# A spectral filter and a gated FFN in one kernel: DRAM scratch rows in another order, forward slabs stored at once and put closer, block-product sums on VectorE

## The chip, the cores and the metric

The kernel runs on one core of one Trainium2 chip. The metric is device time in microseconds of one execution. The kernel before took 199.49 us as the median of three runs (199.12 to 199.73). The engines are named as in the profile: PE is TensorE (matmuls), PEld its weight loads, DVE is VectorE, ACT is ScalarE, POOL is GpSimd, and SP is SyncE, whose queue issues nearly all DMAs here.

## The reference: what is computed

```python
x  = A_x                                   # [1, 2048, 640] bf16
xn = layernorm(x)                          # over the last axis
X  = rfft2(xn) * (w_r + 1j * w_i)          # w_r, w_i: [2048, 321]
s  = irfft2(X)                             # [1, 2048, 640]
g  = silu((gelu(xn @ w_gate) * (xn @ w_up)) @ w_down)   # 640 -> 1536 -> 640
return x + s * g
```

## The kernel before, in words

The 2048 rows are 16 slabs (`NS`) of 128 rows: row = 16 * n2 + n1, with n1 the slab and n2 the partition. The spectral branch is a chain of matmuls with Fourier matrices.

- *Forward.* For each slab, `slab_S1` transforms along n2 (five matmuls into a PSUM tile `pz`, copied to SBUF by ScalarE), and `slab_D` transforms along the 640 columns (matmuls into `pd`, copied by ScalarE into one of six buffers of `RZ`). `slab_D` then stores the slab to the DRAM scratch `ZDR` (line 604).
- *Stage 2* needs the values of all 16 slabs for each frequency row, so `load_B2` reads `ZDR` back in another order, in ten loads (`B2`). `s2_in` transforms over the slabs (matmuls into `px`, line 647), ScalarE copies the result (`xs`, line 655), VectorE multiplies it by the two weights `W1` and `W2` into `RZ` (line 659). `s2_out` transforms back (matmuls into `pu`, line 674), ScalarE copies the result into `RX` in two parts (line 680), and after every second burst the rows are stored to the DRAM scratch `UDR` (line 683). There are eleven such bursts.
- *Inverse.* `load_V` reads `UDR` back as slabs (`VY` for the first four, `W2` for the rest, line 699). `gather` copies some columns (`vr`, line 710), `slab_S1i` transforms along n2 (`pv`, line 730), `group_Di` along the columns (`pd`, lines 575 and 579), VectorE forms the output rows, and `finish` multiplies by the gate, adds x and stores.

The FFN works on four groups of 512 rows. `ffn_half` is five matmuls of 512 columns with the gate weights (`psg`, then a gelu on ScalarE, line 811) or the up weights (`psu`, then a product on VectorE into `UT`, line 813). The down product of groups 1 and 2, and of half of group 3, is done with seven block products instead of eight per pair of row blocks (`product`, line 900): `u_sum` and `w_sum` form sums of blocks beforehand on VectorE, and behind each product the partial results are added (line 907). The other down products are plain (`down_third`, line 944). `gated` turns a down product into the gate, for groups 1 and 2 with a tanh on ScalarE and a multiply on VectorE, which is emitted one and two products later (`flush`).

`w_plus` and `w_minus` load the filter weights row by row into `W1` and `W2`.

The order of the work is written out by hand. The list `back` holds 144 steps of FFN work; `plan[s]` holds what is emitted right behind step s, by `put`. Steps 36 to 59 are the halves of FFN group 1 (even steps gate, odd steps up), 60 to 71 its block products (seven sixths of a product to a step), 72 to 95 and 96 to 107 the same of group 2, 108 to 131 the halves of group 3, 132 to 137 its block products, 138 to 143 the last plain ones. Every engine runs its own instructions in the order in which they are emitted, and the SP queue its DMAs. PSUM has two banks each for `psg` and `psu`, and two buffers of two banks shared by `pz`, `pd`, `px`, `pu` and `pv`.

Of the kernel before, what the change touches and what calls it, by code (L numbers as in the profile page):

```python
# [10 lines left out]
BF16 = mybir.dt.bfloat16  # L11
# [3 lines left out]
P = 128  # L15
# [17 lines left out]
def kernel(  # L33
# [27 lines left out]
    ZDR = dram.tile([2, 2, NS, 64, L], BF16)  # L61
    UDR = dram.tile([2, 2, NS, 64, L], BF16)
# [14 lines left out]
def build(nc, env):  # L77
# [32 lines left out]
    def w_plus(i, hh, lo):  # L110
        WT, sp = spw[i]
        p0 = hh * 64
        u0 = lo * 32 + hh * 16
        nc.sync.dma_start(out=WT[p0:p0 + 61:4, lo].rearrange("p h l -> p (h l)"),
                          in_=sp[:, u0:u0 + NS, :].rearrange("k h l -> k (h l)"))

    def w_minus(i, hh, lo):
        WT, sp = spw[i]
        p0 = hh * 64 + 1
        u0 = lo * 32 + hh * 16  # L120
        if u0 == 0:
            nc.sync.dma_start(out=WT[p0:p0 + 61:4, lo, 1:NS, :], in_=sp[:, 127:112:-1, :])
            nc.sync.dma_start(out=WT[p0:p0 + 61:4, lo, 0, :], in_=sp[:, 64, :])
        else:
            nc.sync.dma_start(out=WT[p0:p0 + 61:4, lo, :, :], in_=sp[:, 128 - u0:112 - u0:-1, :])
# [145 lines left out]
    def affine(name, src, a, b):  # L271
# [4 lines left out]
    kh_f, hi_f, s_f, h_f, pf, n1_f, z_f = bits(  # L276
        "pb", [(1, 31), (6, 1), (0, 31), (5, 1), (0, 127), (1, 15), (0, 1)])
# [14 lines left out]
    u64 = fma("u64", e64, 64.0, fma("u_f", z_f, 32.0, kh_f))  # L292
# [299 lines left out]
    def slab_D(n1):  # L592
# [10 lines left out]
        for a in range(2):  # L603
            nc.sync.dma_start(out=ZDR[a, :, n1].rearrange("c p l -> p c l"), in_=zd[a:P:2, :, 0:L])

# [9 lines left out]

    def load_B2():
        B2 = big.tile([P, NH, L], BF16, tag="sB", name="B2")
        zv = ZDR.rearrange("a c n (z k h) l -> (a c n z) k h l", z=2, k=2)
        B4 = B2.rearrange("p (k h) l -> p k h l", k=2)
        for h0, h1 in ((0, 3), (3, 6), (6, 9), (9, 12), (12, 16)):  # L620
            for hh in range(2):
                nc.sync.dma_start(out=B4[:, hh, h0:h1, :], in_=zv[:, hh, h0:h1, :])
# [3 lines left out]
        st_b["u"] = RX.rearrange("p b l -> p (b l)")[:, 0:2 * n_u].rearrange("p (s k x) -> p s k x", s=2, k=2)  # L626
# [11 lines left out]
    def s2_in(b):  # L638
# [3 lines left out]
        for lo in range(2):  # L642
            r = slice(64 * lo, 64 * lo + 64)
            for hh in range(2):
                for i, j, kind in s2_tiles(b, lo, hh):
                    ps = px[64 * hh:64 * hh + 64, lo, i * w:j * w].rearrange("p (h l) -> p h l", l=w)
                    nc.tensor.matmul(ps, lhsT=MG[r, kind, 0, :],  # L647
                                     rhs=B2[r, 16 * hh + h0 + i:16 * hh + h0 + j, l0:l0 + w], start=(i == 0),
# [13 lines left out]
    uv = UDR.rearrange("a c n (z k h) l -> (a c n z) k h l", z=2, k=2)  # L662

    def s2_out(b):
# [11 lines left out]
        us = st_b["u"][:, h0 // 3 % 2, :, 0:n * L].rearrange("p k (h l) -> p k h l", l=L)  # L676
# [4 lines left out]
        if l0 + w == L:  # L681
            for hh in range(2):
                nc.sync.dma_start(out=uv[:, hh, h0:h0 + n, :], in_=us[:, hh, :, :])
# [7 lines left out]
    def load_V():  # L691
# [4 lines left out]
        for V, n0, n1 in ((Va, 0, VA), (Vb, VA, NS)):  # L696
            for c in range(2):
                for a in range(2):
                    nc.sync.dma_start(out=V[a:P:2, :, c * L:c * L + L],
                                      in_=UDR[a, c, n0:n1].rearrange("n p l -> p n l"))  # L700
# [182 lines left out]
    TB = 3  # L883
# [7 lines left out]
    def product(g, a, i):  # L891
        if (a, i) == (0, 0):
# [4 lines left out]
                    (A(1, 0), TS[:, 2]), (S[:, 0], TS[:, 0]), (A(0, 1), B4[:, :, 1, 1, :]), (A(1, 1), TS[:, 3]))[i]  # L897
# [9 lines left out]
        add = lambda eng, out, in0, in1: eng.tensor_tensor(out=out, in0=in0, in1=in1, op=ALU.add)  # L907
# [3 lines left out]
        elif i == 1:  # L911
            c = temp()
            add(nc.vector, c, d["p1"], ps)
            gated(g, j, 0, c, True)
        elif i == 2:
            add(nc.vector, d["p1"], d["p1"], ps)
        elif i == 3:
            d["p7"], d["u3"] = temp(), temp()
            nc.scalar.copy(out=d["p7"], in_=ps)  # L919
            add(nc.gpsimd, d["u3"], d["p1"], d["p7"])  # L920
        elif i == 4:
            d["u4"] = temp()
            add(nc.vector, d["u4"], d["p1"], ps)
            add(nc.gpsimd, d["p7"], d["u4"], d["p7"])
        elif i == 5:
            add(nc.vector, d["p1"], d["u4"], ps)
# [133 lines left out]
    for i, at in enumerate((51, 52, 54, 56)):  # L1060
        put(at, w_sum, i)
    put(52, u_sum, nc.vector, 1, 0, 0, 3)
    put(57, u_sum, nc.vector, 1, 1, 0, 3)
    put(59, u_sum, nc.vector, 1, 0, 3, 6)
    for a, at in ((0, 86), (1, 92)):
        put(at, u_sum, nc.vector, 2, a, 0, 3)
    put(95, u_sum, nc.vector, 2, 0, 3, 6)
    put(122, u_sum, nc.vector, 3, 0, 0, 3)
    put(131, u_sum, nc.vector, 3, 0, 3, 6)
    F0 = 30  # L1070
# [21 lines left out]
    sb = z_end + 8  # L1092
# [5 lines left out]
    put(sb + 22, s2_out, len(BURSTS) - 1)  # L1098
    sb += 23
    put(sb, load_V)  # L1100
    vs0 = sb + 8
# [4 lines left out]
    for i, (n0, n) in enumerate(DG):  # L1106
# [3 lines left out]
        d = a + 6 if n == 3 else a + 3  # L1110
# [55 lines left out]
```

## Time and profile before

| | before |
|---|---|
| median of 3 runs | 199.49 us (199.12 to 199.73) |
| profiled execution | 198.94 us |
| its span, first to last instruction | 197.2 us |
| granted TensorE clock | 1.000 |
| busy VectorE / ScalarE / GpSimd | 158.4 / 127.6 / 48.9 us |
| moved by DMA | 32.44 MB |

In the lists of waits a row reads: engine and line that waited, what it waited for, then total us, how often, and the longest. In the timeline a row reads: start and length in us, engine, line, operation, output and inputs, and in brackets how long the engine had been idle in front of it and for what. Rows that begin with a stretch (82.00:95.00) give the length of the stretch and then the busy us of PE, PEld, DVE, ACT and POOL, the granted clock, the share of the DMA engines and GB/s. DMA rows end with KB of one and the median us from issue to landing.

### The profile page before, as it was taken

The page shows a single profiled execution, that of the slowest core. Times are in us where ns is not written, and L with a number is a line of the kernel's source. Part 1 is how long each engine was busy: PE and PEld are TensorE (multiplying, and loading weights), DVE is VectorE, ACT ScalarE, POOL GpSimd, SP SyncE. Part 2 cuts the span into 40 slices and gives each one's busy share as a digit, 9 for nine tenths or more (in the row PEclk, how much of TensorE's full clock was granted, in tenths as well). Part 3 has the DMA queues.
Part 4 walks back from the last instruction along what each step waited for, and adds up shares of the span by engine and source line. Part 5 has one row for each costly group of instructions (what it writes and reads, how often), then busy time and mean ns, then how long its engine had stood idle before and what let it go on. Part 6 is the DMA issues. An engine that isn't in the chain of part 4 may idle for free.

```text
span 197.2 us, 4191 instructions
## 1 busy us (share of the span) xinstructions
PE 188.7 (96%) x1496; PEld 116.4 (59%) x1511; DVE 158.4 (80%) x380; ACT 127.6 (65%) x229; POOL 48.9 (25%) x78
## 2 busy tenths in 40 slices
PE   7999999999999999999899999997999999999992
PEld 5798854777555555676433433454765555557672
DVE  7887888989899877697786658566779887978994
ACT  4668567866976666825598878622766738374761
POOL 4448588997210200032200000002120000000310
PEclk9999999999999999999999999999999999999999
DMA  6999999676596773329953222329910416040713
GB/s 162 301 331 362 367 320 188 139 207 208 134 179 126 218 243 104 99 72 317 243 132 103 76 100 100 116 69 257 325 41 28 138 41 195 33 136 15 220 44 94
DMA packets 39653, 32.44 MB, mean 165 GB/s; under 512 B 13264, under 2 KB 38608, under 8 KB 39376
## 3 DMA queue, kind: packets, MB, share of 16 engines
q1 hardware_dynamic: 37568, 29.87, 54.7%
q10 hardware_dynamic: 1968, 0.98, 1.8%
q0 software_dynamic: 96, 1.31, 1.7%
q8 instruction: 12, 0.20, 0.4%
q14 instruction: 9, 0.07, 0.1%
HBM read 19.03 MB, written 7.88 MB: 136 GB/s over the span
## 4 chain that ended last, share of the span: by engine, by line
PE 81%; DVE 8%; DMA 3%; issue 3%; ACT 2%; SPq 1%; DVEq 0%; ACTq 0%
PE psg L806 26%; PE psu L806 25%; PE psu L900 5%; PE psg L900 5%; PE psu L944 3%; PE psg L944 3%; PE pz L565 2%; PE pu L674 2%; PE pv L730 2%; PE pd L596 2%; PE pd L575 2%; DMA VY<-UDR 2%; PE px L647 2%; DMA X<-in_A_x_dram 2%; DVE X L788 1%
## 5 line engine op out<-in xcount | busy, mean ns | idle before, releaser
L806 PE MATMUL psg<-XG,Wg 128*128 128x512 bf16 (+2 forms) x282 | 60.1, 342 | 0.7 <-issue 0.3
L806 PE MATMUL psu<-XG,Wu 128*128 128x512 bf16 (+2 forms) x283 | 60.2, 342 | 0.4 <-issue 0.2
L813 DVE TENSOR_TENSOR UT<-psu,ge 128x512 bf16<-128x512 f32 (+2 forms) x58 | 34.4, 593 | 18.4 <-PE psu L806 16.1
L811 ACT ACTIVATE ge<-psg 128x512 bf16<-128x512 f32 (+2 forms) x58 | 30.3, 523 | 16.8 <-PE psg L806 16.1
L806 PEld LDWEIGHTS <-Wu 128*128 128x128 bf16 x290 | 27.0, 98 | 22.4
L806 PEld LDWEIGHTS <-Wg 128*128 128x128 bf16 x290 | 25.9, 98 | 21.3 <-issue 3.5
L659 DVE TENSOR_TENSOR RZ<-xs,W 128x972 bf16<-128x972 bf16 (+2 forms) x22 | 14.0, 678 | 5.5 <-ACT xs L655 4.7
L900 PEld LDWEIGHTS <-UT 128*128 128x128 bf16 x150 | 14.3, 98 | 5.6 <-issue 0.2
L944 PEld LDWEIGHTS <-UT 128*128 128x128 bf16 x156 | 14.4, 98 | 5.0
L601 ACT CAST RZ<-pd 128x660 bf16<-128x660 f32 x16 | 11.3, 707 | 9.1 <-PE pd L598 9.1
L190 DVE BATCH_NORM_STATS2 st<-X 128x6 f32<-128x320 bf16 x32 | 14.0, 476 | 0.4 <-DMA X<-in_A_x_dram 0.4
L732 ACT CAST W<-pv 128x640 bf16<-128x640 f32 x16 | 11.0, 688 | 5.0 <-PE pv L730 4.8
L755 ACT ACTIVATE W<-pd 128x960 bf16<-128x960 f32 (+2 forms) x14 | 10.0, 778 | 5.1 <-PE pd L579 5.1
L680 ACT CAST RX<-pu 128x486 bf16<-128x486 f32 (+4 forms) x22 | 12.2, 557 | 0.3
L655 ACT CAST xs<-px 128x972 bf16<-128x972 f32 (+2 forms) x11 | 10.3, 935 | 3.2 <-PE px L647 3.2
L944 PE MATMUL psg<-Wd,UT 128*128 128x320 bf16 (+1 forms) x84 | 11.8, 288 | 0.0
L567 ACT CAST GEN<-pz 128x640 bf16<-128x640 f32 x16 | 11.2, 698 | 0.0
L907 POOL TENSOR_TENSOR Tfwd<-Y,XG 128x320 f32<-128x320 f32 x1 | 0.9, 868 | 40.0 <-ACT XG L919 40.0
L844 ACT ACTIVATE th<-Tfwd 128x320 f32<-128x320 f32 x10 | 4.5, 469 | 9.5 <-DVE Tfwd L907 9.5
L907 POOL TENSOR_TENSOR Tfwd<-XG,Tfwd 128x320 f32<-128x320 f32 x1 | 0.9, 857 | 38.3 <-ACT Tfwd L919 38.3
L944 PE MATMUL psu<-Wd,UT 128*128 128x320 bf16 (+1 forms) x72 | 10.3, 290 | 0.0
L761 DVE TENSOR_TENSOR W<-W 128x960 bf16<-128x960 bf16 (+1 forms) x12 | 7.3, 632 | 1.8 <-ACT W L755 1.8
(215 smaller groups left out, 317.1 us busy)
## 6 DMA issues: line engine op xcount, KB each, us to landing
ZDR<-RZ SPq DMA_DIRECT2D x32, 80.2 KB, 2.8
UDR<-RX SPq DMA_DIRECT2D x10, 240.8 KB, 2.4
RX<-in_A_x_dram SPq DMA_DIRECT2D x14, 160.0 KB, 2.6
B<-ZDR SPq DMA_DIRECT2D x8, 240.8 KB, 4.3
W<-UDR SPq DMA_DIRECT2D x4, 481.5 KB, 7.1
X<-in_A_x_dram SPq DMA_DIRECT2D x3, 640.0 KB, 10.0
Wd<-in_B_w_down_dram SPq DMA_DIRECT2D x1, 1920.0 KB, 14.3
out_dram<-VY SPq DMA_DIRECT2D x12, 160.0 KB, 1.8
```

The source lines that it names most:

```text
L190: nc.vector.bn_stats(out=st_n[n1][:, k, :], in_=X[:, n1, 320 * k:320 * k + 320])
L567: nc.scalar.copy(out=Zt[n1], in_=pz)
L601: nc.scalar.copy(out=zd.rearrange("p c (q e) -> p c q e", e=10), in_=pd[:, :, 0:330].rearrange("p c (e q) -> p c q e", q=33))
L655: nc.scalar.copy(out=xs, in_=px[:, :, 0:n * w].rearrange("p k (h l) -> p k h l", l=w))
L659: nc.vector.tensor_tensor(out=pp[-1], in0=xs, in1=WT[:, :, h0:h0 + n, l0:l0 + w], op=ALU.mult)
L680: nc.scalar.copy(out=us[:, :, :, c0:c0 + (w + 1 - m) // 2], in_=pv[:, :, :, m:w:2])
L732: nc.scalar.copy(out=vs, in_=pv)
L806: nc.tensor.matmul(ps, lhsT=WT[:, c, t * P:(t + 1) * P], rhs=xnT[g][:, c, c0:c1_], start=(c == 0), stop=(c == 4))
L811: nc.scalar.activation(out=ges[t], in_=ps, func=ACT.Gelu_apprx_tanh)
L813: nc.vector.tensor_tensor(out=UT[:, t, c0:c1_], in0=ps, in1=ges[t], op=ALU.mult)
L900: nc.tensor.matmul(ps, lhsT=lhs[:, t, :], rhs=rhs[:, t, :], start=(t == 0), stop=(t == 5))
L944: nc.tensor.matmul(ph, lhsT=UT[:, t, j * P:(j + 1) * P], rhs=Wd[:, t, c0:c1_], start=(t == 0), stop=(t == NT - 1))
```

## The change

- The scratches `ZDR` and `UDR` lose the dimension that split odd and even rows. A scratch row index is now sign, half, row (`z a k`), so what stage 2 reads for one half lies together. A slab is stored by one transfer instead of two. `load_B2` and the `UDR` stores move 64 partitions with rows twice as long, instead of 128 partitions; `load_V` uses four transfers of 128 partitions instead of eight of 64.
- The constant `u64` and the weight loads follow the new order: `w_plus` now reads every second row, 16 pieces for a partition, where it read one long piece. `s2_in` reads every second row of `B2`. The two halves of the `RX` store buffer change places.
- The forward slabs (`FA`) stand closer behind step 43; the last `slab_D` and `load_B2` move from step 60 to 56. Stage 2 starts at step 67 instead of 68, `load_V` stays at 91, and the inverse starts at `vs0` = 98 instead of 99.
- In `product`, the fourth and fifth product change places. ScalarE's copy of one product and the two adds on GpSimd go; VectorE makes seven adds per pair instead of five.
- The sums in front of the products (`u_sum`) are made for five of six tiles at once before the last two halves, and for one tile behind them, instead of three and three.

```diff
-    ZDR = dram.tile([2, 2, NS, 64, L], BF16)
-    UDR = dram.tile([2, 2, NS, 64, L], BF16)
+    ZDR = dram.tile([2, NS, P, L], BF16)
+    UDR = dram.tile([2, NS, P, L], BF16)
...
-        u0 = lo * 32 + hh * 16
-        nc.sync.dma_start(out=WT[p0:p0 + 61:4, lo].rearrange("p h l -> p (h l)"),
-                          in_=sp[:, u0:u0 + NS, :].rearrange("k h l -> k (h l)"))
+        u0 = lo * 32 + hh
+        nc.sync.dma_start(out=WT[p0:p0 + 61:4, lo], in_=sp[:, u0:u0 + 31:2, :])
...
-    u64 = fma("u64", e64, 64.0, fma("u_f", z_f, 32.0, kh_f))
+    u64 = fma("u64", e64, 64.0, fma("u_f", h_f, 32.0, s_f))
...
-        for a in range(2):
-            nc.sync.dma_start(out=ZDR[a, :, n1].rearrange("c p l -> p c l"), in_=zd[a:P:2, :, 0:L])
+        nc.sync.dma_start(out=ZDR[:, n1].rearrange("c p l -> p c l"), in_=zd[:, :, 0:L])
...
+    def turned(t, lo, h0, h1):
+        return t[64 * lo:64 * lo + 64, 2 * h0:2 * h1, :].rearrange("p k l -> p (k l)")
+
+    def rows(t, lo, h0, h1):
+        v = t.rearrange("c n (z a k) l -> a (c n z) (k l)", a=2, z=2)
+        return v[lo, :, 2 * h0 * L:2 * h1 * L]
...
-            for hh in range(2):
-                nc.sync.dma_start(out=B4[:, hh, h0:h1, :], in_=zv[:, hh, h0:h1, :])
+            for lo in range(2):
+                nc.sync.dma_start(out=turned(B2, lo, h0, h1), in_=rows(ZDR, lo, h0, h1))
...
-                                     rhs=B2[r, 16 * hh + h0 + i:16 * hh + h0 + j, l0:l0 + w], start=(i == 0),
+                                     rhs=B2[r, 2 * (h0 + i) + hh:2 * (h0 + j) - 1 + hh:2, l0:l0 + w], start=(i == 0),
...
-        us = st_b["u"][:, h0 // 3 % 2, :, 0:n * L].rearrange("p k (h l) -> p k h l", l=L)
+        ut = st_b["u"][:, (h0 // 3 + 1) % 2, 0:2 * n, :]
+        us = ut.rearrange("p (h k) l -> p k h l", k=2)
...
-            for hh in range(2):
-                nc.sync.dma_start(out=uv[:, hh, h0:h0 + n, :], in_=us[:, hh, :, :])
+            for lo in range(2):
+                nc.sync.dma_start(out=rows(UDR, lo, h0, h0 + n), in_=turned(ut, lo, 0, n))
...
-                for a in range(2):
-                    nc.sync.dma_start(out=V[a:P:2, :, c * L:c * L + L],
-                                      in_=UDR[a, c, n0:n1].rearrange("n p l -> p n l"))
+                nc.sync.dma_start(out=V[:, :, c * L:c * L + L], in_=UDR[c, n0:n1].rearrange("n p l -> p n l"))
...
-    TB = 3
+    TB = 5
...
-                    (A(1, 0), TS[:, 2]), (S[:, 0], TS[:, 0]), (A(0, 1), B4[:, :, 1, 1, :]), (A(1, 1), TS[:, 3]))[i]
+                    (S[:, 0], TS[:, 0]), (A(1, 0), TS[:, 2]), (A(0, 1), B4[:, :, 1, 1, :]), (A(1, 1), TS[:, 3]))[i]
...
         elif i == 3:
-            d["p7"], d["u3"] = temp(), temp()
-            nc.scalar.copy(out=d["p7"], in_=ps)
-            add(nc.gpsimd, d["u3"], d["p1"], d["p7"])
+            d["u4"] = temp()
+            add(d["u4"], d["p1"], ps)
         elif i == 4:
-            d["u4"] = temp()
-            add(nc.vector, d["u4"], d["p1"], ps)
-            add(nc.gpsimd, d["p7"], d["u4"], d["p7"])
+            c, d["u3"] = temp(), temp()
+            add(c, d["u4"], ps)
+            gated(g, j + 1, 1, c, True)
+            add(d["u3"], d["p1"], ps)
...
         elif i == 6:
-            add(nc.vector, d["u3"], d["u3"], ps)
-            gated(g, j + 1, 1, d["p7"], True)
+            add(d["u3"], d["u3"], ps)
             gated(g, j + 1, 0, d["u3"], True)
...
-    for i, at in enumerate((51, 52, 54, 56)):
+    for i, at in enumerate((51, 52, 53, 54)):
         put(at, w_sum, i)
...
+    for g, at in ((1, 56), (2, 92), (3, 128)):
+        put(at, u_sum, nc.vector, g, 0, 0, TB)
+        if g in STR:
+            put(at + 1, u_sum, nc.vector, g, 1, 0, TB)
+        put(at + 3, u_sum, nc.vector, g, 0, TB, 6)
...
-    FA = (29, 31, 33, 35, 37, 39, 41, 43, 45, 47, 49, 51, 53, 55, 57, 58)
+    FA = (29, 31, 33, 35, 37, 39, 41, 43, 44, 46, 47, 49, 50, 51, 53, 54)
     for n1 in range(NS):
-        put(min(FA[n1] + 2, 45 + n1), slab_D, n1)
+        put(FA[n1] + 2, slab_D, n1)
         put(FA[n1], slab_S1, n1)
-    z_end = F0 + 30
+    z_end = FA[NS - 1] + 2
...
-    sb = z_end + 8
+    sb = 67
...
-    put(sb + 22, s2_out, len(BURSTS) - 1)
-    sb += 23
+    put(sb + 23, s2_out, len(BURSTS) - 1)
+    sb += 24
     put(sb, load_V)
-    vs0 = sb + 8
+    vs0 = sb + 7
...
-        d = a + 6 if n == 3 else a + 3
+        d = a + 6 if n == 3 else a + 4
```

More of the change, by code (lines that the diff above doesn't have):

```diff
@@ L119, in w_minus @@
         p0 = hh * 64 + 1
-        u0 = lo * 32 + hh * 16
+        u0 = lo * 32 + hh
         if u0 == 0:
-            nc.sync.dma_start(out=WT[p0:p0 + 61:4, lo, 1:NS, :], in_=sp[:, 127:112:-1, :])
+            nc.sync.dma_start(out=WT[p0:p0 + 61:4, lo, 1:NS, :], in_=sp[:, 126:97:-2, :])
             nc.sync.dma_start(out=WT[p0:p0 + 61:4, lo, 0, :], in_=sp[:, 64, :])
         else:
-            nc.sync.dma_start(out=WT[p0:p0 + 61:4, lo, :, :], in_=sp[:, 128 - u0:112 - u0:-1, :])
+            nc.sync.dma_start(out=WT[p0:p0 + 61:4, lo, :, :], in_=sp[:, 128 - u0:97 - u0:-2, :])
     def w_twin(i, pm):
@@ L274, in affine @@
         return t
-    kh_f, hi_f, s_f, h_f, pf, n1_f, z_f = bits(
-        "pb", [(1, 31), (6, 1), (0, 31), (5, 1), (0, 127), (1, 15), (0, 1)])
+    hi_f, s_f, h_f, pf, n1_f, z_f = bits("pb", [(6, 1), (0, 31), (5, 1), (0, 127), (1, 15), (0, 1)])
     cs_f = h_f
@@ L660, in s2_in @@
         st_b[b] = pp
-    uv = UDR.rearrange("a c n (z k h) l -> (a c n z) k h l", z=2, k=2)
     def s2_out(b):
@@ L906, in product @@
         j = 2 * a
-        add = lambda eng, out, in0, in1: eng.tensor_tensor(out=out, in0=in0, in1=in1, op=ALU.add)
+        add = lambda out, in0, in1: nc.vector.tensor_tensor(out=out, in0=in0, in1=in1, op=ALU.add)
         if i == 0:
```

19 lines of the change are left out of this document (4 added, 15 removed).

## The prediction

> **What bounds the kernel now.** I read the page first, then TensorE's waits, then the timeline around each wait.
>
> ```profile
> span 197.2 us, 4191 instructions
> ...
> PE 188.7 (96%) x1496; PEld 116.4 (59%) x1511; DVE 158.4 (80%) x380; ACT 127.6 (65%) x229; POOL 48.9 (25%) x78
> ```
> ```profile
> PE pv L730 <- DMA VY<-UDR: 1.3, 1, 1.3
> ...
> PE pu L674 <- ACT RX L680: 0.8, 2, 0.5
> ...
> PE pd L575 <- ACT W L732: 0.2, 1, 0.2
> ```
>
> TensorE is busy for 188.7 of 197.2 us. The change leaves its matmuls as they are, so a gain can only come out of TensorE's waits. Three of those lie near the change: 1.3 us for V (the slabs read back from UDR), 0.8 us where stage 2 opens, 0.2 us in the tail. A gain is at most 2.3 us, about 1.2%; a loss has no such bound.
>
> Two stretches of the timeline serve as rulers, one of stage 2 running and one where the inverse begins:
>
> ```profile
> 107.70 0.40 PE L647 MATMUL px<-B,MG 64*64 64x477 bf16 x4
> ...
> 108.15 0.96 ACT L655 CAST xs<-px 128x954 bf16<-128x954 f32 x1 [0.48 <-PE px L647]
> ...
> 109.14 1.23 DVE L659 TENSOR_TENSOR RZ<-xs,W 128x954 bf16<-128x954 bf16 x2 [0.57 <-ACT xs L655]
> ...
> 110.07 0.60 ACT L811 ACTIVATE ge<-psg 128x512 bf16<-128x512 f32 x1
> ...
> 110.71 0.40 PE L647 MATMUL px<-B,MG 64*64 64x486 bf16 x4
> ...
> 110.94 0.57 PE L674 MATMUL pu<-RZ,N 64*64 64x477 bf16 x8
> ```
>
> ```profile
> 133.71 0.98 PE L900 MATMUL psg<-X,XG 128*128 128x320 bf16 x6
> 134.53 0.22 PE L730 MATMUL pv<-Tinv,VY 128*128 128x128 bf16 x1
> 136.03 0.33 PE L730 MATMUL pv<-Tinv,VY 128*128 128x128 bf16 x3 [1.29 <-DMA VY<-UDR]
> ```
>
> A burst of stage 2 takes 3.01 us (107.70 to 110.71); px and pu fill 0.80 of it (110.71 to 111.51), so the two FFN halves between take 1.1 us each. A block product takes 0.82 us (133.71 to 134.53).
>
> **The change part by part.** The sums are made against the profiled execution, 198.94 us, which lies 0.55 us below the median of the runs shown (199.49). The difference is put on the median at the end.
>
> *Forward slabs closer, one store each.*
>
> ```profile
> 79.61 0.70 ACT L567 CAST GEN<-pz 128x640 bf16<-128x640 f32 x1
> ...
> 80.37 0.60 ACT L811 ACTIVATE ge<-psg 128x512 bf16<-128x512 f32 x1
> ```
> ```profile
> 82.65 0.41 PE L596 MATMUL pd<-FT,GEN 128*128 128x132 bf16 x4
> ...
> 83.17 0.71 ACT L601 CAST RZ<-pd 128x660 bf16<-128x660 f32 x1
> ```
> ```profile
> 72.91 12.41 SPq L604 DMA_DIRECT2D ZDR<-RZ  x16
> 87.38 4.79 SPq L622 DMA_DIRECT2D B<-ZDR  x10
> ```
> ```profile
> B<-ZDR SPq DMA_DIRECT2D x8, 240.8 KB, 4.3
> ```
> ```profile
> 90.38 0.79 PE L647 MATMUL px<-B,MG 64*64 64x162 bf16 x5
> ```
>
> The last slab's matmul (slab_D of 15) moves from step 60 to step 56. That is one product and three FFN halves earlier on TensorE, so about 4 us: it would run near 78.9 instead of 82.65. In the dense stretch ScalarE evicts two banks per slab (0.71 and 0.70) and a gelu every second step (0.60). From step 49 to 56 that is 11 evictions and 4 gelus, 10.2 us, beside about 12 us of TensorE; it fits, and the two PSUM buffers are each free before their next use. The tightest place is slab 12's first matmul group, which needs the last fold just as VectorE ends it: 0 to 0.2 us lost, I take 0.1.
>
> SyncE issues the old stores back to back, 16 in 12.41 us, so 0.6 to 0.8 us each and partly waiting. Sixteen fewer in all free about 10 us of that queue, which is off the path. The last store then leaves at about 80 and the first load of B2 at about 83 instead of 87.38. A landing of 4.3 gives 87.9 for the first pair. px of burst 0 moves one product earlier, to about 89.5, so the cover is 1.6 us: price nothing. If that cover goes, px waits, and everything behind it on TensorE.
>
> The weights' w_plus loads become 256 rows of 642 bytes in place of 16 long ones. They are read first in stage 2, tens of us later: nothing.
>
> *Stage 2 opens one step earlier, with all sums on VectorE.*
>
> ```profile
> 82.00:95.00 13.00, 13.00 (x110) 8.93 (x108) 11.19 (x24) 5.84 (x12) 3.10 (x4) 1.00 0.60 188
> ```
> ```profile
> 91.55 0.95 ACT L655 CAST xs<-px 128x972 bf16<-128x972 f32 x1
> ...
> 92.53 1.91 DVE L659 TENSOR_TENSOR RZ<-xs,W 128x972 bf16<-128x972 bf16 x2 [0.80 <-DMA B<-ZDR]
> ...
> 94.76 0.47 DVE L907 TENSOR_TENSOR FT<-Tfwd,psu 128x320 f32<-128x320 f32 x1
> ...
> 95.95 0.47 ACT L844 ACTIVATE th<-Tfwd 128x320 f32<-128x320 f32 x1 [3.13 <-DVE Tfwd L907]
> ...
> 96.33 0.94 ACT L655 CAST xs<-px 128x954 bf16<-128x954 f32 x1
> ...
> 97.16 1.17 ACT L680 CAST RX<-pu 128x486 bf16<-128x486 f32 x2
> ...
> 98.38 0.60 PE L674 MATMUL pu<-RZ,N 64*64 64x159 bf16 x10 [0.51 <-ACT RX L680]
> ```
>
> Before, ScalarE stood 3.13 us in front of a tanh whose sum VectorE had not made. xs of burst 1 (96.33) sat behind it, RX of burst 0 behind that, and pu at 98.38 waited for the buffer. Per pair of row blocks the change takes one 320-wide copy from ScalarE and two adds from GpSimd, and gives VectorE two adds more (seven for five). In the stretch 82 to 95 VectorE has 11.19 of 13 us, and gets 4 adds x 0.47 = 1.9 us. About 0.8 us of u_sum work moves ahead of it, since five sixths instead of one half is formed before the products. That makes 12.3 of 13: nearly full.
>
> I follow the new order: px of burst 0 ends near 90.3, xs (0.95) and the two multiplies (1.23, as in the bursts that run) end near 92.8; pu of burst 0 stands three products after px, near 93.1, and need not wait. xs of burst 1 has one tanh in front of it, whose sum is made by then, so the old wait goes. What is late next is burst 2. In front of its xs stand RX (to 95.5), three tanh (3 x 0.47) and a gelu (0.60), two of the tanh behind sums that VectorE makes after burst 1's multiplies. xs of burst 2 starts at 97.5 to 98.4, and its multiplies end at 99.7 to 100.6. Its pu is due near 99.6. The stall is 0.1 to 1.0 us against 0.8 before; I take 0.8, the end where sums do lag as they did, so no change. Bounds for the part: a gain of 0.8, or a loss of 1.9 if all the added VectorE time lands on the path.
>
> *Stage 2 running.*
>
> In the rows of the running bursts xs starts 0.45 after px; the multiplies end at 110.37, 0.57 before pu at 110.94. With the shift by one step, px stands behind a gate half instead of an up half. So ScalarE does the gelu (0.60) before xs, which starts about 0.65 after px, 0.2 later. The slack falls from 0.57 to about 0.37 and the period stays: price 0. Each 0.1 us beyond the slack would cost 0.1 in each of nine bursts.
>
> *V.*
>
> ```profile
> 126.51 1.47 SPq L683 DMA_DIRECT2D UDR<-RX  x1
> 130.57 2.62 SPq L699 DMA_DIRECT2D VY<-UDR  x4
> ```
> ```profile
> VY<-UDR SPq DMA_DIRECT2D x4, 160.5 KB, 3.1
> ```
>
> TensorE reaches the inverse at 134.53 and stands 1.29 us for the last of four loads, each about 0.65 us of issue (2.62 / 4). The change makes two of the four, so the last goes out about 1.3 us earlier; each carries twice the bytes, which gives part of it back (0.3 to 0.6). Burst 9's UDR store also leaves one step earlier and no longer runs into burst 10's, whose second issue took 1.47 us. That may bring the first load forward by up to 1 us. Against this the inverse starts one product earlier (134.53 - 133.71 = 0.82). V comes 0.7 to 2.0 earlier than it did, the need 0.82 earlier; but a wait of 1.29 that starts 0.82 earlier and ends 0.7 to 2.0 earlier still means TensorE goes on 0.7 to 1.29 earlier. I take 1.0. Bounds: 0 if loads land no sooner, 1.29.
>
> The copies of V into vr stand one product earlier in VectorE's queue and block it until V lands. TensorE has four banks to run ahead into, and only one product lies between: nothing.
>
> *Tail.*
>
> ```profile
> 179.35 0.36 DVE L881 TENSOR_TENSOR XG<-UT 128x384 bf16<-128x384 bf16 x1
> ...
> 180.28 0.49 DVE L788 TENSOR_TENSOR VY<-VY,XG 128x640 bf16<-128x640 bf16 x1
> ...
> 182.14 0.55 DVE L881 TENSOR_TENSOR UT<-UT,XG 128x768 bf16<-128x768 bf16 x1
> ...
> 185.69 0.87 POOL L907 TENSOR_TENSOR Tfwd<-Y,XG 128x320 f32<-128x320 f32 x1 [40.04 <-ACT XG L919]
> 185.87 1.21 DVE L770 TENSOR_TENSOR X<-W 128x960 bf16<-128x960 bf16 x1
> 186.21 0.46 PE L575 MATMUL pd<-FI,W 128*128 128x160 bf16 x4 [0.15 <-ACT W L732]
> ```
> ```profile
> 180.00:190.00 10.00, 9.85 (x95) 7.02 (x93) 9.76 (x22) 6.73 (x13) 2.03 (x2) 1.00 0.39 115
> ```
>
> VectorE has 9.76 of 10 us here, TensorE 9.85: both carry the tail. After the last gelu product the change adds two adds (0.95). It shortens three u_sum pieces: between 384 and 768 elements an operation grows by 0.19, so 128 elements cost about 0.23, three save 0.4. One slab's finish (two of 0.49) falls ahead of it, as the inverse is one step earlier. An add on GpSimd beside which an operation took 1.21 us is gone; how much of that it caused I leave out. The sum is about -0.4, so VectorE follows TensorE. The wait of 0.15 goes too, since ScalarE loses a copy in front of that eviction.
>
> **Sum:** forward +0.1, stage 2 0, V -1.0, tail -0.15: -1.05 us. On the profiled execution that is 197.9; on the median 199.49 - 1.05 = 198.4.
>
> **The rivals.**
>
> 1. *No measurable change.* The loads of V land no sooner, because they carry the same bytes and start behind the same last store. Then only 0.1 to 0.5 us is left: 199.0 to 199.8. For it: the four old loads were issued within 2.62 us and the last landed 3.1 after, so size may rule rather than count. Against it: two loads are issued in half the time.
>
> 2. *All three waits go.* -2.2 us, 197.3. For it: GpSimd's adds, ScalarE's copy and the tanh queue in front of xs are lighter. Against it: VectorE is full there.
>
> 3. *Slower, by transfers over half the partitions.* B2's loads now fill 64 partitions each, with rows twice as long. If their landing doubles (8.6 instead of 4.3), the first pair, issued at 83 to 83.6, lands at 92.2, px of burst 0 waits 2.7 us, and the UDR stores slow V too: about 201.5. It decides from a landing of 5.9 on. For it: the cover is only 1.6 us. Against it: the first pair has the queue to itself. [...]
>
> 4. *Slower, by VectorE where stage 2 opens.* If the sums lag more than about 1 us beyond my chain, xs and the multiplies of bursts 0 to 2 all come late and the 1.9 us land on the path: 199.49 - 1.05 + 1.9 = 200.3.
>
> **How the numbers follow.** The forecast's own case 0.38, with 197.9 to 198.9 (V's bounds); rival 1 0.20; rival 2 0.12; rival 3 0.12; rival 4 0.18. A change under 0.3%, 0.6 us, cannot be told from none here. Faster: 0.38 + 0.12 = 0.50. Same: 0.20. Slower: 0.30. The range must hold 8 in 10: from below rival 2's 197.3 to beyond rival 4's 200.3, leaving out most of rival 3: 197.1 to 200.8.
>
> **What would show it.** Right: TensorE's wait at pv under 0.5 us; a wait of about 0.8 us at pu of burst 2 and none at pu of burst 1; bursts still 3.01 us apart; px of burst 0 waiting for no DMA; no wait in the dense slabs. Wrong: a wait of px on B2 (rival 3); waits of more than 1.5 us around the first three bursts, or a period above 3.1 (rival 4); a wait at pv still above 1 us (rival 1).

## The result and the profile after

The changed kernel takes 196.54 us (median of four runs, 196.30 to 197.35) beside 199.31 us (199.00 to 199.73): a ratio of 0.9867, interval 0.9832 to 0.9902, 2.8 us faster. The forecast of 198.4 had the direction and less than half of the size; the time lies below the range. On three other chips the same kernel later gave 0.9946, 0.9897 and 0.9927. The mean of the four ratios is 0.991, about 1.8 us, so the first measurement was the most favourable one. The other three ratios, times 199.49, give 197.4 to 198.4, inside the forecast's range: that the time fell below the range is owed in part to the chip that was measured. A step of the prediction was wrong all the same (see below). Of the traced executions used later, one (no_layout) had a granted clock of 0.991 and took 200.47 us, 2.7 above that kernel's median; it is not read.

The profiled execution is the one of 197.35 us, the slowest of the four. The head of its page, and TensorE's waits in it (total us, times, longest):

```profile
span 195.6 us, 4175 instructions
...
PE 188.2 (96%) x1496; PEld 116.1 (59%) x1511; DVE 159.9 (82%) x391; ACT 126.6 (65%) x224; POOL 40.1 (20%) x68
```
```profile
PE pu L674 <- ACT RX L681: 0.4, 1, 0.4
PE pv L729 <- DMA VY<-UDR: 0.4, 1, 0.4
...
PE pz L563 <- DMA Tfwd<-Tinv: 0.3, 1, 0.3
```

The wait at pv fell from 1.3 to 0.4 us, that at pu from 0.8 to 0.4, and pd's is gone. A wait of 0.3 at pz, in the forward part, is new. GpSimd lost 8.8 us of work, VectorE took on 1.5.

The timeline where stage 2 opens (start, us, engine, line, operation; in brackets the idle time before it and what ended it):

```profile
89.84 0.41 PE L649 MATMUL px<-B,MG 64*64 64x162 bf16 x5
...
92.72 0.40 PE L649 MATMUL px<-B,MG 64*64 64x159 bf16 x5
...
93.18 0.96 ACT L657 CAST xs<-px 128x954 bf16<-128x954 f32 x1 [1.45 <-PE px L649]
...
94.70 1.23 DVE L661 TENSOR_TENSOR RZ<-xs,W 128x954 bf16<-128x954 bf16 x2
...
96.51 0.57 PE L674 MATMUL pu<-RZ,N 64*64 64x159 bf16 x10
...
98.91 1.16 ACT L681 CAST RX<-pu 128x480 bf16<-128x480 f32 x2
...
100.13 0.63 PE L674 MATMUL pu<-RZ,N 64*64 64x486 bf16 x8 [0.44 <-ACT RX L681]
```

Three things differ from before. px of burst 0 takes 0.41 us for its five matmuls, where it took 0.79. xs of burst 1 starts as px ends, with ScalarE idle in front of it, where it stood behind a tanh. pu of burst 1 (96.51) does not wait; the only wait left is at pu of burst 2.

The timeline at the start of the inverse, and in the tail:

```profile
128.60 1.11 SPq L699 DMA_DIRECT2D VY<-UDR  x2
...
132.97 0.22 PE L729 MATMUL pv<-Tinv,VY 128*128 128x128 bf16 x1
133.61 0.34 PE L729 MATMUL pv<-Tinv,VY 128*128 128x128 bf16 x3 [0.43 <-DMA VY<-UDR]
```
```profile
183.57 0.98 PE L899 MATMUL psg<-X,UT 128*128 128x320 bf16 x6
...
184.39 0.45 PE L573 MATMUL pd<-FI,W 128*128 128x160 bf16 x4
184.76 0.25 PE L577 MATMUL pd<-FI,W 32*128 32x160 bf16 x4
185.05 1.79 PE L942 MATMUL psg<-Wd,UT 128*128 128x320 bf16 x12
```

The two loads of V are issued 2 us earlier (128.60 for 130.57), the inverse starts 1.6 us earlier (132.97 for 134.53). pd follows its product after 0.82 us, where it was 1.14 before (186.21 - 185.07).

**One ledger for all traces.** The list of waits leaves out short losses. So I took, from each trace, the time between the starts of two successive matmuls, less the usual time for a matmul of that form, and summed it by stretch. "Early" is 6 to 42 us, "stage 2" 88 to 130 (some 2 us of it is a regular pause of about 0.2 in each burst), "pv" 130 to 138, "tail" from 176. In the traces that miss matmul records (the first of both kernels among them) a missing record looks like a loss of 0.2; only traces with all 1511 are in the table, but for the kernel before, whose values have the missing ones taken out (stage 2: the 3.17 of again3 plus 1.02, by which it falls behind that trace between the product at 87.84 and the FFN half at 126.14). The ledger leaves out the first 6 us and what follows the last matmul.

| kernel | ratio to before, same chip | early | stage 2 | pv | tail |
|---|---|---|---|---|---|
| before | 1 | 0.3 | 4.2 | 1.58 | 0.99 |
| layout alone | 0.9987 [0.9971, 1.0004] | 0.30 | 4.26 | 0.87 | 0.98 |
| sums alone | 0.9936 [0.9915, 0.9956] | 0.43 | 3.84 | 1.69 | 0.66 |
| places alone | 0.9959 [0.9940, 0.9979] | 0.43 | 3.47 | 1.22 | 0.66 |
| no_sums | 0.9917 [0.9890, 0.9943] | 0.33 | 3.48 | 0.32 | 0.66 |
| changed, again | 0.9946 [0.9928, 0.9965] | 0.69 | 3.17 | 0.91 | 0.75 |
| changed, again3 | 0.9927 [0.9898, 0.9956] | 0.32 | 3.17 | 0.45 | 0.75 |
| b2_late | 0.9903 [0.9879, 0.9928] | 0.61 | 3.17 | 0.00 | 0.75 |
| s2_late | 0.9958 [0.9937, 0.9978] | 0.57 | 3.77 | 0.43 | 1.45 |
| first_v | 0.9905 [0.9880, 0.9929] | 0.32 | 3.16 | 0.00 | 0.75 |
| before_no_v | 0.9947 [0.9926, 0.9968] | 0.62 | 4.46 | 0.00 | 0.98 |
| after_no_v | 0.9874 [0.9856, 0.9892] | 1.09 | 3.16 | 0.00 | 0.75 |

The stretches stage 2 and tail repeat to 0.01 us wherever the code there is the same and no transfer is waited for; early and pv do not, since they hang on transfers. From before to the changed kernel (again3) the gain is 1.0 in stage 2, 1.1 at pv and 0.24 in the tail. For the first pair of traces it is 1.0, 0.76 and 0.24, less 0.34 lost early, chiefly at pz; their spans differ by 1.6 us.

### The profile page after: what moved, and what is told of

Read it like the earlier page. It is cut to its first block, busy times and chain, and to the rows that moved or that the text cites. A ratio compares the mean times of both kernels' runs of the same rounds, so it can differ in the third digit from the quotient of the medians.

```text
span 195.6 us, 4175 instructions
## 1 busy us (share of the span) xinstructions
PE 188.2 (96%) x1496; PEld 116.1 (59%) x1511; DVE 159.9 (82%) x391; ACT 126.6 (65%) x224; POOL 40.1 (20%) x68
## 4 chain that ended last, share of the span: by engine, by line
PE 84%; DMA 7%; SPq 2%; DVE 2%; ACT 2%; issue 1%; DVEq 0%; ACTq 0%
PE psu L805 26%; PE psg L805 25%; PE psg L942 5%; PE psg L899 4%; PE psu L942 4%; PE psu L899 3%; DMA B<-ZDR 3%; PE psg L609 2%; PE pz L563 2%; DMA VY<-UDR 2%; PE pd L573 2%; PE pv L729 2%; SPq L624 2%; PE pd L594 2%; PE pu L674 2%
## 5 line engine op out<-in xcount | busy, mean ns | idle before, releaser
L805 PEld LDWEIGHTS <-Wu 128*128 128x128 bf16 x290 | 26.1, 98 | 22.5 <-issue 3.4
L805 PEld LDWEIGHTS <-Wg 128*128 128x128 bf16 x290 | 26.6, 98 | 20.1 <-issue 0.2
L661 DVE TENSOR_TENSOR RZ<-xs,W 128x972 bf16<-128x972 bf16 (+2 forms) x22 | 13.3, 648 | 9.8 <-ACT xs L657 9.5
L942 PEld LDWEIGHTS <-UT 128*128 128x128 bf16 x156 | 14.5, 98 | 5.1
L681 ACT CAST RX<-pu 128x486 bf16<-128x486 f32 (+4 forms) x22 | 12.3, 560 | 0.3
L942 PE MATMUL psg<-Wd,UT 128*128 128x320 bf16 (+1 forms) x84 | 11.8, 288 | 0.0
L942 PE MATMUL psu<-Wd,UT 128*128 128x320 bf16 (+1 forms) x72 | 10.3, 291 | 0.0
L207 POOL TENSOR_TENSOR rst<-ve,mhalf 128x1 f32<-128x1 f32 (+1 forms) x6 | 5.5, 913 | 11.5 <-DVE ve L205 11.5
L899 PE MATMUL psu<-Wd,UT 128*128 128x320 bf16 x48 | 7.8, 300 | 0.0
L594 PEld LDWEIGHTS <-GEN 128*128 128x128 bf16 x64 | 5.1, 98 | 3.3
## 6 DMA issues: line engine op xcount, KB each, us to landing
UDR<-RX SPq DMA_DIRECT2D x10, 240.8 KB, 3.1
B<-ZDR SPq DMA_DIRECT2D x8, 240.8 KB, 5.1
```

What stands on the lines that cost most here:

```text
L661: nc.vector.tensor_tensor(out=pp[-1], in0=xs, in1=WT[:, :, h0:h0 + n, l0:l0 + w], op=ALU.mult)
L681: nc.scalar.copy(out=us[:, :, :, c0:c0 + (w + 1 - m) // 2], in_=pv[:, :, :, m:w:2])
L805: nc.tensor.matmul(ps, lhsT=WT[:, c, t * P:(t + 1) * P], rhs=xnT[g][:, c, c0:c1_], start=(c == 0), stop=(c == 4))
L899: nc.tensor.matmul(ps, lhsT=lhs[:, t, :], rhs=rhs[:, t, :], start=(t == 0), stop=(t == 5))
L942: nc.tensor.matmul(ph, lhsT=UT[:, t, j * P:(j + 1) * P], rhs=Wd[:, t, c0:c1_], start=(t == 0), stop=(t == NT - 1))
```

## The experiments

The diff has three parts that can be taken alone: *layout* (the scratch's order, the one-transfer stores and loads), *sums* (the body of `product`, `TB`, the places of `w_sum` and `u_sum`) and *places* (`FA`, `z_end`, `sb`, `vs0`, `d`).

**Each part alone, beside the changed kernel.** Edits against the kernel before, cut to a line or two each:

```diff
 layout
-    ZDR = dram.tile([2, 2, NS, 64, L], BF16)
+    ZDR = dram.tile([2, NS, P, L], BF16)
...
 sums
-            add(nc.gpsimd, d["u3"], d["p1"], d["p7"])
+            add(d["u3"], d["p1"], ps)
...
 places
-    sb = z_end + 8
+    sb = 67
...
```

> The changed kernel once more, for its spread and a second trace. The runs seen so far are 197.35 (the profiled one), 196.30, 196.58 and 196.49. Theory: the profiled run was held up once, by the wait of 0.3 us of pz on the turned matrix (0.42 us against the kernel before) and by a longer wait at pv (0.4); a second trace then shows neither, a span of 194.5 to 195.0, and a time of 196.3 to 196.7. Rival: these waits are always there and only the other runs differ by chance; then the trace shows the two waits again and a span near 195.6.

> The kernel before with the DRAM layout alone: one store for a forward slab, loads of B2 and V in two transfers over 64 partitions; places and sums as before. Theory (the gain came from fewer transfers on SyncE's queue): the loads of B2 go out before 85 in place of 87.4, the hidden wait in px of burst 0 (0.79 us for 0.41) goes, 0.4 us; V's loads end sooner, 0.5 to 1.3 us; together 0.9 to 1.7 us faster, 197.6 to 198.4. Rival A (the same bytes land no sooner, the gain came from the places and sums): within 0.3 us of the kernel before. Rival B (half the partitions are slower): slower than the kernel before by more than 0.3 us.

> The kernel before with the sums alone: every add on VectorE, the new order of products, the new pieces of u_sum; layout and places as before. Theory: the tail's wait of 0.2 us at pd and VectorE's 0.4 us there give 0.25; where stage 2 opens the waits at pu fall from 0.8 to 0.4 or stay; together 0.2 to 0.7 us faster, 198.6 to 199.1. Rival (VectorE becomes the bound there): a wait of more than 1 us at pu, 199.6 or more.

> The kernel before with the places alone: the last forward slabs closer, B2's loads after the last of them, stage 2 and the inverse one step earlier; two stores for a slab and the old sums stay. Theory: the loads of B2 still stand behind 32 store issues, so they go out at 84 to 87 and px of burst 0, which now runs earlier, waits 0 to 1.5 us for them; the wait for V grows by the 0.8 us that the inverse is earlier, net nothing: 199.0 to 200.3. Rival (the places made the gain): 1 us or more faster, 198.3 or less.

Measured: again 197.58 us, layout 198.37, sums 197.08, places 197.85, beside 198.35 for the kernel before on that chip. The trace of again is as its rival said, with both waits and a span of 195.7, but its times (196.90 to 198.05) are 1 us above those of the first chip, which neither theory said. For the layout alone its rival A is right, in time: nothing measurable, though its trace shows 0.7 us less at pv. The sums gained 1.3 us by the medians, almost twice the most that their theory allowed; their traced execution, the slowest of nine, has a span only 0.9 us under that of the kernel before. The places did more than their theory, less than the rival. On this chip the sums alone (197.08) came out faster than the whole change (197.58), though the intervals of the two ratios overlap.

In the layout's trace (timeline), the last matmuls of px of burst 0 stand by themselves, because TensorE waited in front of them:

```profile
90.21 0.40 PE L649 MATMUL px<-B,MG 64*64 64x162 bf16 x3
90.99 0.40 PE L649 MATMUL px<-B,MG 64*64 64x486 bf16 x2 [0.38 <-DMA B<-ZDR]
```

This is the 0.79 us of the kernel before, seen apart: a wait for B2 of 0.4 us which a group of matmuls had covered up. With the places alone (timeline) it is gone, and pu of burst 1 no longer waits either; what is left is pu of burst 2:

```profile
89.59 0.40 PE L647 MATMUL px<-B,MG 64*64 64x162 bf16 x5
...
96.26 0.57 PE L674 MATMUL pu<-RZ,N 64*64 64x159 bf16 x10
...
100.19 0.63 PE L674 MATMUL pu<-RZ,N 64*64 64x486 bf16 x8 [0.66 <-ACT RX L680]
```

By the ledger the places alone are worth 0.7 us in stage 2, the sums alone 0.4. But most of the sums' 0.4 is a transfer: their px of burst 0 takes 0.52 us in place of 0.79. Behind it they gain nothing at the old places, as their timeline shows:

```profile
90.45 0.52 PE L647 MATMUL px<-B,MG 64*64 64x162 bf16 x5
...
98.63 0.60 PE L674 MATMUL pu<-RZ,N 64*64 64x159 bf16 x10 [0.66 <-ACT RX L680]
```

By the starts, 0.83 us are lost at this pu of burst 1 and 0.38 at px of burst 2; the kernel before loses 0.68 and 0.47 at the pu of bursts 1 and 2. With the changed places the sums are worth 0.3 (no_sums below). Each of the two parts alone also takes the tail from 0.99 to 0.66.

**Without V, and without one part each.** The first two load V from a scratch that was written long before, so that TensorE does not wait for it (the output is then of other data); the others undo one part of the change. The edit for V, as made to the changed kernel:

```diff
-                      in_=UDR[c, n0:n1].rearrange("n p l -> p n l"))
+                      in_=ZDR[c, n0:n1].rearrange("n p l -> p n l"))
...
-    put(sb, load_V)
+    put(sb - 2, load_V)
```

> The kernel before, with V loaded from ZDR (the same bytes, written long before) in place of UDR and issued in front of the last burst's store, so that TensorE cannot wait for it; the output of the inverse is then of other data. Theory: the wait of 1.3 to 1.4 us at pv goes, nothing else changes: 1.2 to 1.4 us faster than the kernel before, ratio 0.993 to 0.994, and runs that lie closer together. Rival (the wait only moves to the copies or the next slab): less than 0.5 us faster, with a new wait at pv or pd.

> The changed kernel with the same edit: V from ZDR, issued before the last burst's store. Theory: its wait of 0.4 to 0.5 us at pv goes. If the change without V is worth what the traces show (stage 2 opening 1.0, tail 0.25, against 0.4 lost at the turned matrix), this kernel is 0.8 to 1.0 us faster than the kernel before with the same edit, and 0.4 to 0.5 us faster than the changed kernel. Rival (V was all of it): the two kernels without the wait agree within 0.3 us.

> The changed kernel with the sums as before: p7's copy on ScalarE, two adds per pair on GpSimd, the old order of products and pieces of u_sum. Theory (the places made room where stage 2 opens, the layout made it for V, the sums nothing): ratio within 0.0015 of the changed kernel's on this chip, a wait at pu of 0.4 to 0.8 us, pd's wait of 0.2 us back. Rival (the sums carry the gain, as their run alone suggests, 1.27 us): 0.8 us or more slower than the changed kernel.

> The changed kernel with the layout as before: two stores per forward slab, four transfers for V, loads over all partitions at stride two. Theory (the layout's share is V's): pv waits 1.3 to 2.1 us in place of 0.5, 0.8 to 1.2 us slower than the changed kernel; the wait at the turned matrix is gone, 0.4 back; net 0.4 to 0.8 us slower than the changed kernel. Rival (the layout is worth nothing, as its run alone says): within 0.3 us of the changed kernel or faster.

Measured: before_no_v 197.43, after_no_v 196.23, no_sums 196.71, no_layout 197.76, beside 198.68. before_no_v gained what its theory said, 1.25 us by the medians (0.9947 by the ratio), though its px waited 0.2 us longer for B2. The two kernels without a wait for V differ by 1.2 us, more than the 0.8 to 1.0 of the theory, which denies the rival that V was all of it: about 1 us of the change has nothing to do with V. no_layout has 0.9961 (0.9935 to 0.9987), some 1.0 us behind the mean of the changed kernel's ratios. So the layout seems to be worth something beside the other two parts, which it was not alone; this is not shown, since no run of the changed kernel stood beside it on that chip, and one of its ratios (0.9946) lies within the interval. no_sums had no wait at pv on TensorE's list (the ledger has 0.32 there), and none at pd, which its theory had back; its waits were that on the first norm, which every trace has, and that at pu of burst 2:

```profile
PE psg L609 <- DVE eps L229: 1.2, 1, 1.2
PE pu L674 <- ACT RX L681: 0.7, 1, 0.7
```

**The changed kernel a third time, two parts undone, and the inverse later.**

```diff
 v_later
-    vs0 = sb + 7
+    vs0 = sb + 8
```

> The changed kernel a third time, beside three of its relatives on one chip. So far its ratio to the kernel before was 0.9867 on one chip and 0.9946 on another; both of its traces show the waits at pv (0.4, 0.5 us) and at the turned matrix (0.3, 0.2). Theory (how much it gains hangs on whether these waits for transfers occur in a run): a ratio between 0.987 and 0.995, and a trace whose gain over the trace of before is 1.4 to 1.7 us with both waits, 2.3 to 2.6 us with neither. Rival (the chips differ, the waits are always there): both waits in the trace, and a ratio near one of the two.

> The changed kernel with the old sums again, now beside the changed kernel. It measured 0.9917 of the kernel before, with no wait at pv and none at the turned matrix. Theory (the sums are worth 0.2 us at most): within 0.5 us of the changed kernel. Rival (the sums cost, since VectorE's adds delay the eviction of the last burst and so V's loads by 0.2 to 0.4 us): 0.5 us or more faster than the changed kernel.

> The changed kernel with the places as before: forward slabs, B2's loads, stage 2 and the inverse at their old steps; layout and sums changed. Theory (the places made the gain where stage 2 opens, 0.7 us, and the earlier inverse makes nothing or 0.4): 0.6 to 1.1 us slower than the changed kernel; the hidden wait of px for B2 and the waits at pu of 0.7 us are back. Rival (layout and sums suffice): within 0.3 us of the changed kernel.

> The changed kernel with the inverse one step later (one number), so that one more product of 0.82 us lies between the loads of V and pv. Theory (pv still waits 0.4 to 0.5 us there, and the tail has room): no wait at pv, 0.3 to 0.5 us faster than the changed kernel. Rival (the tail pays): pd waits 0.2 us or more for ScalarE again, or the last output leaves later, and it is within 0.2 us or slower.

Measured, beside 198.91: again2 196.71 (0.9897, interval 0.9871 to 0.9923), no_sums2 196.74 (0.9896), no_places 197.35 (0.9922, 0.9901 to 0.9942), v_later 196.40 (0.9874, 0.9847 to 0.9900). The ratio of again2 lies in the range of its theory, and its span is 2.3 us under that of the kernel before. Its trace is neither of the two cases of the theory, for it has pz's wait and not pv's. Two rows of its waits:

```profile
PE pu L674 <- ACT RX L681: 0.4, 1, 0.4
PE pz L563 <- DMA Tfwd<-Tinv: 0.4, 1, 0.4
```

pv's wait comes and goes between executions of one kernel (0.4, 0.5, none), pz's too. With it the span is 195.6 or 195.7 us, without it 194.9. The places: 0.6 us by the medians, though the intervals overlap, and the waits that their theory named are back:

```profile
PE px L649 <- DMA B<-ZDR: 0.6, 1, 0.6
PE pu L674 <- ACT RX L681: 0.5, 1, 0.5
```

The sums undone cost nothing in time here (196.74 beside 196.71): their 0.3 us in stage 2 is less than these runs can tell. v_later has no wait at pv, but pays with a new one in the tail, at a down product and not at pd, where its rival had put it (`PE psg L942 <- DVE Tfwd L906`, 0.3 us); it is 0.3 us faster by the medians, within the intervals.

**What of the places opens stage 2, and pv alone.**

```diff
 b2_late
-    put(z_end, load_B2)
+    put(z_end + 4, load_B2)
 s2_late
-    sb = 67
+    sb = 68
 first_v
-            put(a + ((1, 2, 4)[k] if n == 3 else 1), slab_S1i, n0 + k)
+            put(a + ((1 + (i == 0), 2, 4)[k] if n == 3 else 1), slab_S1i, n0 + k)
```

> The changed kernel beside three one-line edits of it, as their reference. So far 0.987 to 0.995 of the kernel before. Its trace should show 0.6 us lost at pu of burst 2, and either a wait of 0.4 to 0.5 us at pv or none.

> The changed kernel with the loads of B2 at their old step, four later; all else as changed. Theory (half of the gain where stage 2 opens is px of burst 0 no longer waiting for B2): the loads leave near 87 in place of 83.4, land near 91, px of burst 0, due at 89.8, waits 0.4 to 1.5 us, and the kernel is slower than the changed one by that. Rival (the loads have room either way): no wait at px, within 0.2 us of the changed kernel.

> The changed kernel with stage 2 and all behind it one step later, as before; the loads of B2 stay early. Theory (the step matters by the order on ScalarE: xs of burst 1 stands in front of the tanh at the changed step and behind it at the old one): pu of burst 1 waits 0.5 to 0.7 us again, that of burst 2 less than 0.4, and the opening loses 0.1 to 0.5 us against the changed kernel. Rival (only B2's loads mattered): no wait at pu of burst 1, the opening as in the changed kernel within 0.1 us.

> The changed kernel with the first inverse slab's pv one product (0.82 us) later, beside the second slab's; everything else at its step. Theory (pv's wait of 0 to 0.5 us goes, and the tail keeps its 0.25 us, of which the kernel with the whole inverse later lost some): no wait at pv, none in the tail, 0.2 to 0.6 us faster than the changed kernel. Rival (two slabs' pv back to back make a new wait, at ScalarE's eviction or at pd): within 0.2 us.

Measured, beside 198.56: again3 197.00, b2_late 196.44, s2_late 197.43, first_v 196.56. b2_late did not do what it was to do. Its loads leave where they did in again3, at 83.12 in place of 82.68 (timeline of SyncE's queue):

```profile
80.12 0.36 SPq L601 DMA_DIRECT2D ZDR<-RZ  x1
83.12 6.27 SPq L624 DMA_DIRECT2D B<-ZDR  x10
```

They wait for the last slab's store to land, not for their turn in the order: from the issue of that store (80.12 + 0.36) to the first load lie 2.6 us, and for the same loads in the first trace of the changed kernel the list of waits of SyncE's queue has `SPq L624 <- DMA ZDR<-RZ`, 2.4 us. So the loads of B2 left earlier because the last slabs were put closer, and the step of their own, four earlier, is worth nothing.

s2_late tells the other half. With B2 early and stage 2 at its old step px of burst 0 takes 0.41 us, but pu of burst 1 waits again and px of burst 2 as well (waits):

```profile
PE pu L674 <- ACT RX L681: 0.7, 1, 0.7
...
PE psg L942 <- DVE Tfwd L906: 0.6, 1, 0.6
PE px L649 <- ACT xs L657: 0.3, 1, 0.3
```

The opening loses 0.60 us against the changed kernel (3.77 for 3.17), by the order on ScalarE that its theory named, and a little more than it named. Its timeline has xs of burst 1 behind the tanh again:

```profile
96.36 0.47 ACT L843 ACTIVATE th<-Tfwd 128x320 f32<-128x320 f32 x1 [0.52 <-DVE Tfwd L906]
96.74 0.94 ACT L657 CAST xs<-px 128x954 bf16<-128x954 f32 x1
```

The tail loses 0.7 more, at the first down product, whose sum VectorE makes late: with the changed places (`d = a + 4`) the tail wants the inverse at its new step.

first_v has no wait at pv and none in the tail, the shortest span of all (194.3 us), and its times, 196.56 beside 197.00 for the changed kernel, lie on the side its theory named (0.4 us), though the intervals overlap.

**Which of the sums' edits counts.**

```diff
-            add(nc.gpsimd, d["u3"], d["p1"], d["p7"])
+            add(nc.vector, d["u3"], d["p1"], d["p7"])
...
-            add(nc.gpsimd, d["p7"], d["u4"], d["p7"])
+            add(nc.vector, d["p7"], d["u4"], d["p7"])
```

> The changed kernel with the old sums, in the old order and with ScalarE's copies, but the two adds per pair that GpSimd made are made by VectorE (two words). Theory (GpSimd's adds hold up VectorE's multiplies of two SBUF operands: 1.90 us in place of 1.24 in the kernel with the old sums): every multiply of the opening takes 1.24, and the loss at pu of burst 2 falls from 0.8 towards the 0.6 us of the changed kernel; equal to the changed kernel within 0.3 us. Rival (the order of the sums made it): the multiply is short, but pu of burst 2 still loses 0.8 us or more, since VectorE now has the adds as well.

> The kernel before with the same two words changed. Theory: the multiply of burst 0 takes 1.24 us in place of 1.91, the one in the tail 0.65 in place of 1.21; the opening gains 0 to 0.4 us, the tail 0.2 to 0.3. Rival (VectorE, with 0.95 us more of adds per pair, falls behind): pu of burst 1 waits longer than 0.7 us, and the kernel is no faster than before.

Measured, beside 198.57: eng_new 197.85 (0.9961, 0.9941 to 0.9981), eng_old 199.96 (1.0073, 1.0050 to 1.0097). The multiplies are short in both, and no time is gained: eng_old is 1.4 us slower than the kernel before, and eng_new's ratio lies above all four of the changed kernel, which did not run on that chip. By the starts pu of burst 2 loses 0.82 us in eng_new, as in no_sums. Of no_sums, of eng_new, and of eng_old, the timelines:

```profile
93.74 1.90 DVE L661 TENSOR_TENSOR RZ<-xs,W 128x954 bf16<-128x954 bf16 x2 [0.31 <-ACT xs L657]
93.83 1.29 POOL L906 TENSOR_TENSOR Tfwd<-FT,Tfwd 128x320 f32<-128x320 f32 x1
```
```profile
94.45 1.22 DVE L661 TENSOR_TENSOR RZ<-xs,W 128x954 bf16<-128x954 bf16 x2
...
100.05 0.63 PE L674 MATMUL pu<-RZ,N 64*64 64x486 bf16 x8 [0.66 <-ACT RX L681]
```
```profile
92.46 1.24 DVE L659 TENSOR_TENSOR RZ<-xs,W 128x972 bf16<-128x972 bf16 x2 [0.86 <-DMA B<-ZDR]
...
98.35 0.60 PE L674 MATMUL pu<-RZ,N 64*64 64x159 bf16 x10 [0.66 <-ACT RX L680]
```

The add that ran on GpSimd delays one multiply by 0.66 us; on VectorE it takes 0.49 itself, twice. That is a bad trade in the tail, where eng_new and eng_old get a wait of 0.3 to 0.4 us for a sum, and more so behind the last matmul, where the ledger does not look. The last twelve matmuls and the last VectorE operation (timelines), of the kernel before and of eng_old:

```profile
192.66 0.83 PE L944 MATMUL psg<-Wd,UT 128*128 128x128 bf16 x12
194.23 0.22 DVE L789 TENSOR_TENSOR X<-X,RX 128x128 bf16<-128x128 bf16 x1
```
```profile
192.83 0.83 PE L944 MATMUL psg<-Wd,UT 128*128 128x128 bf16 x12
195.16 0.23 DVE L789 TENSOR_TENSOR X<-X,RX 128x128 bf16<-128x128 bf16 x1
```

TensorE ends 0.17 us later, VectorE 0.93: with the two adds more it has not caught up when the outputs are due. So the theory of the engine falls and its rival stands. What the sums gain must then come from what the change does beside it: the new order of products and pieces of u_sum, and adds straight from PSUM without ScalarE's copy. This is by exclusion; these were not tried apart.

## Why the prediction was right and wrong

Most of its signs of being right came out: pv's wait at 0.5 us or under, no wait at pu of burst 1, bursts 3.0 us apart, px of burst 0 waiting for no DMA, no wait in the dense slabs. Wrong was the price of one step.

- **Forward slabs, "+0.1": right, and half read.** No trace loses anything between 42 and 82 us, and B2's loads left at 83.42, as the prediction had it. "Price nothing" was wrong: the kernel before already lost 0.4 us to those loads, at px of burst 0. The row quoted in that very paragraph shows it (0.79 us for five matmuls that take 0.40), and so does VectorE's 0.80 idle behind B2; I read the first as work.
- **"Stage 2 opens one step earlier", 0: the step that failed.** Measured: 1.0 us gained, outside the bound of 0.8. Three errors lie in it. The loss before was not 0.8 but about 1.6 us: 0.4 at px of burst 0, and at pu 0.68 and 0.47 by the starts of the matmuls, where the list of waits says 0.5 and 0.3. For the stall at burst 2 (named rightly, as the only one left) I took 0.8 out of 0.1 to 1.0, by what the sums had cost before; 0.6 was measured, 0.4 of it listed. And the bound of the gain was made from the same short list. By parts: stage 2's earlier step 0.6 (s2_late); the closer slabs 0.4 (px in the layout's trace against that of the places); the sums 0.3 (no_sums against again3). They overlap, for the whole is 1.0. VectorE had 11.95 of 13 us between 82 and 95, where 12.3 was worked out.
- **Stage 2 running, 0: right.** Burst to burst it stays at 3.0 us, and the stretch from 105 to 130 changes by no more than 0.1.
- **V, -1.0: right in mechanism and size, but not one number.** 0.7 to 1.4 us (1.58 before; 0.82, 0.91, 0.2 and 0.45 in four traces of the changed kernel). The layout alone has 0.87, so the layout makes most of it. That it is the two loads in place of four, and not the other stores and transfers of the layout, is not shown.
- **Tail, -0.15:** 0.24. The wait went as said. The lost copy on ScalarE, given as its reason, is not needed for it: the places alone, which keep the copy, lose the wait too (0.66).
- **The sum.** 1.0 + 1.1 + 0.24 is 2.4 us against 1.05 (1.6 in the first pair of traces). "A gain is at most 2.3 us" came from a list that leaves short losses out, and was too low by at least the 0.4 at px.
- **The rivals.** The second, that all three waits go, with 197.3 us, came nearest, though of its three waits only pd's went and the others shrank; its objection, that VectorE is full, did not hold. The third's effect is there and small: the same 240.8 KB take longer in the new layout, over 64 partitions, 5.1 us for 4.3, under its threshold of 5.9, and px does not wait. The first and the fourth did not come about: the loss at pv is 0.91 us or less for 1.58, and no burst is late.
- **What stays open.** The first chip's 2.8 us is more than the 2.4 that the ledger finds, and the second's 1.1 is less. Transfers that are late in some executions (pv up to 0.9 us, early losses 0.3 to 1.1, and the end of the span 2.5 to 3.0 us behind VectorE's last operation) are of that size, and the kernel before has them too; which ones those untraced runs had can't be said.

## What to carry to other kernels

Sum the losses from the starts of the instructions before you bound a gain: the five matmuls of px that took 0.79 us for their usual 0.40 held a wait of 0.4, though no list names it. When an instruction is moved by a step, write down the order on every engine it feeds; here 0.6 us of the gain where stage 2 opens came from one cast that passed in front of a tanh on ScalarE. Follow the other engines past the last matmul too: in eng_old VectorE ended 0.9 us later, and no wait of TensorE shows it. The wait for V, whose cover was near zero, wasn't a number but a spread of 0.2 to 0.91 us over four traces of one kernel, and a single pair of runs may show either end.

## What was not expected of the hardware

Transfers of the same size over 64 partitions in place of 128 landed later. Rows of the issues (KB each, median us from issue to landing), of the places alone and of the changed kernel:

```profile
UDR<-RX SPq DMA_DIRECT2D x10, 240.8 KB, 2.3
...
B<-ZDR SPq DMA_DIRECT2D x8, 240.8 KB, 4.0
```
```profile
UDR<-RX SPq DMA_DIRECT2D x10, 240.8 KB, 3.1
...
B<-ZDR SPq DMA_DIRECT2D x8, 240.8 KB, 5.1
```

That is 0.8 to 1.1 us more for each, on both ways. The layout also doubles the rows and changes their order in the scratch, so the number of partitions was not tried by itself.

A VectorE multiply of two SBUF operands took 1.90 us (no_sums, at 93.74) in place of 1.23 (the changed kernel, at 94.70) for the pair of them when a GpSimd add of SBUF operands started inside it, and the add took 1.29 (at 93.83) in place of 0.89 for the one before it (at 92.86). What makes the two engines hold each other up is not shown. But eng_new (0.9961, beside 0.9917 and 0.9896 for no_sums on other chips) and eng_old (1.4 us slower than the kernel before) show that freeing VectorE of this is worth less than the adds it then has to make itself.
